# The output projections and the q transposes of a decode-attention kernel, regrouped: wider tiles, two PSUM banks, two copying engines

## The chip, the cores and the metric

The kernel runs on one core of one Trainium2 chip. The metric is the device time of one execution, in microseconds (us); lower is better. "Span" is the time between the first and the last instruction in the profile; in the fast runs of most kernels here the device time is 1.2 to 1.3 us longer than the span. Engine names in the profile are PE (TensorE matmuls), PEld (TensorE weight loads), DVE (VectorE), ACT (ScalarE), POOL (GpSimd) and SP (SyncE, which issues the DMAs).

## The reference, cut to what matters

Two independent attention layers, A and B, decode one token for a batch of 8 against a long cache. Their outputs stand side by side.

```python
# per layer: x (8,1,1024), k_cache and v_cache (8,32,4096,128), wq (1024,4096), wo (4096,1024), all bf16
q      = (x @ wq).reshape(B, Sq, H, Dh)            # then (B, H, Sq, Dh)
scores = einsum("bhqd,bhkd->bhqk", q, k_cache) * Dh ** -0.5
p      = softmax(scores)
o      = einsum("bhqk,bhkd->bhqd", p, v_cache)
y      = o.transpose(0, 2, 1, 3).reshape(B, Sq, H * Dh) @ wo      # (8, 1, 1024)
out    = concatenate([y_A, y_B], axis=-1)                        # (8, 1, 2048)
```

Nearly all the traffic is the four caches: the profile counts 1107 MB read from memory.

## The kernel before

A ring of three large buffers in on-chip memory receives tiles of k, v and the weights. VectorE multiplies and folds k tiles, TensorE sums them and applies the probabilities to v. At the head, q is projected and transposed; at the end, the two outputs are projected with `wo`. The change touches only the head and the end.

The transposes of q, four groups of eight rows per layer, each with its own small copy:

```python
def make_qT(c):
    for hb in range(HB):                                   # HB = 4
        rows = slice(32 * hb, 32 * hb + B)
        def emit(e, rows=rows):
            for j in range(HQ):                            # HQ = 8
                i = e.transpose(misc_bf16[:, j * B:(j + 1) * B], q_sb[rows, c, j * Dh:(j + 1) * Dh], ident[rows, rows],
                                tile_position=(rows.start, 0))
            return i
        op = add("pe", emit, [opQs[(c, hb, 0)], opQs[(c, hb, 1)], ...])
        opQT[c] = opQT["last"] = add("dve", ...tensor_copy(...), [op])
```

The output projection. Four column tiles of TensorE work side by side on 256 columns each: in the trace of the first projection four matmuls start every 109 ns at full clock and every 213 ns at half, while one takes 363 ns (the page's mean for this line, both projections). The weights of the second projection arrive in four cuts, of 20, 8, 3 and 1 rows of 4 column tiles, so that only a little work is left after the last cut lands:

```python
wo_cuts = ((0, 20), (20, H - 4), (H - 4, H - 1), (H - 1, H))
...
def make_proj(c):
    w = tile_of("wo", c)
    for i, (r0, r1) in enumerate(wo_cuts if c == NC - 1 else ((0, H),)):
        def emit(e, r0=r0, r1=r1):
            for r in range(r0, r1):
                for q in range(NT):                        # NT = 4, DT = 256
                    col = r * D + q * DT
                    x = e.matmul(proj[32 * q:32 * (q + 1), 0:DT], on_sb[:, c, r:r + H * B:HQ],
                                 w[:, col:col + DT], start=(r == 0), stop=(r == H - 1), tile_position=(0, 32 * q))
            return x
        opProj[c] = add("pe", emit, [opNorm[c], opT[("wo", c, i)], c_pad, opEv.get(c - 1)])
    opEv[c] = add("dve", lambda e: e.tensor_copy(orow[:, c, :], proj[:, 0:DT]), [opProj[c]])
    outs.append(dma(out[...], orow[0:128:32 // B, c, :], ...))
```

Each matmul here is a pair of instructions, a weight load and the matmul itself. The first projection has 128 pairs, the second 128: 80, 32, 12 and 4 in its cuts.

## Time and profile before

| | before |
|---|---|
| device time, median | 2563.53 us |
| span of the profiled execution | 2562.3 us |
| memory traffic | 432 GB/s over the span |
| VectorE busy | 85% |
| last weights landed to end of span | about 2.7 us (2562.3 - 2559.62) |

The page of the profiled execution first gives each engine's busy time and share, then, in 40 equal slices of the span, the busy tenths of the DMA engines. The third kind of line is a group of instructions: line, engine, operation, output and input tile, shape, count | busy us, mean ns of one | idle time just before them, and what ended most of it.

```profile
span 2562.3 us, 18832 instructions
...
PE 1115.7 (44%) x7712; PEld 396.7 (15%) x7712; DVE 2170.6 (85%) x1042; ACT 129.9 (5%) x401; POOL 2.6 (0%) x15
...
DMA  9999999999999999999999999999999999999999
...
L330 DVE TENSOR_TENSOR ring<-ring,qbc 128x8192 bf16<-128x8192 bf16 x256 | 1131.7, 4421 | 310.9 <-DMA ring<-in_A_k_cache_dram 158.0
...
L305 DVE COPY qT<-misc 128x64 bf16<-128x64 bf16 x8 | 3.5, 436 | 17.6 <-PE misc L301 17.6
```

The DMA engines are full in every slice (9 in all 40). VectorE, the busiest compute engine, waits 310.9 us for k tiles, so it has room. The same is read from a long middle stretch, in the view by windows (stretch in us, its length, then busy us and count of PE, PEld, DVE, ACT and POOL; mean granted clock of TensorE, DMA share, GB/s):

```profile
2000.00:2500.00 500.00, 221.85 (x1464) 76.61 (x1462) 436.54 (x208) 23.98 (x77) 0.00 (x0) 0.67 1.00 433
```

At the end, the timeline of TensorE and VectorE (start us, duration us, then the group; in brackets the idle time before it and what ended it):

```profile
2540.13 5.49 PE L431 MATMUL proj<-ring,on_sb 128*32 128x256 bf16 x128 [9.92 <-DMA ring<-in_A_wo_dram]
...
2552.35 4.50 PE L431 MATMUL proj<-ring,on_sb 128*32 128x256 bf16 x80 [6.73 <-DMA ring<-in_B_wo_dram]
...
2557.16 1.22 PE L431 MATMUL proj<-ring,on_sb 128*32 128x256 bf16 x32 [0.31 <-DMA ring<-in_B_wo_dram]
```

Every part of the second projection waits for its cut of weights: TensorE is done with one cut before the next lands. The chain that ended last (start us, us, what) says the same of the very end:

```profile
2519.89 39.72 DMA ring<-in_B_wo_dram
2559.62 0.04 issue
2559.66 0.36 PE proj L431 x4
2560.03 0.02 issue
2560.05 0.42 DVE orow L435
```

The last cut landed at 2559.62 us; four matmuls, one copy of 0.42 us, and the output DMA, issued at 2560.50 us, follow it.

### The profile page before, as it was taken

Reading aid. Unit: us, or ns where it says so; the run is one execution under the profiler, and the core shown is the slowest. Engines: PE = TensorE matmul, PEld = TensorE weight load, DVE = VectorE, ACT = ScalarE, POOL = GpSimd, SP = SyncE. Lnnn points to the kernel's source line nnn. Section 1 sums busy time; section 2 is a strip of 40 time slices with the busy share of each in tenths; the row PEclk is TensorE's granted clock in tenths of the full one; section 3 lists DMA queues with packets and bytes.
Section 4 is the critical chain, followed back from the end, with each engine's and each line's share of the span. In section 5 each row is a group of like instructions: output and inputs, shape, how many; then the busy total and the mean of one; then the engine's idle time right before and its main releaser. Section 6 shows DMA issues by size and latency. Waiting matters only on the chain.

```text
span 2562.3 us, 18832 instructions
## 1 busy us (share of the span) xinstructions
PE 1115.7 (44%) x7712; PEld 396.7 (15%) x7712; DVE 2170.6 (85%) x1042; ACT 129.9 (5%) x401; POOL 2.6 (0%) x15
## 2 busy tenths in 40 slices
PE   2443443443443443444444444434444434434434
PEld 1111111111111111111111111111111111111112
DVE  3898898898898898898898888988988988988983
ACT  1100000000000000000000000000000000000000
POOL 0000000000000000000000000000000000000000
PEclk7676766767767767766666766767667666767667
DMA  9999999999999999999999999999999999999999
GB/s 425 427 438 430 437 431 436 432 436 432 435 431 437 430 438 430 435 432 435 433 431 437 431 435 433 434 433 435 433 435 433 435 433 435 433 435 433 435 433 394
DMA packets 19554, 1107.51 MB, mean 432 GB/s; under 512 B 2184, under 2 KB 2248, under 8 KB 2520
## 3 DMA queue, kind: packets, MB, share of 16 engines
q1 hardware_dynamic: 19512, 1107.34, 99.9%
q8 instruction: 7, 0.11, 0.0%
q10 hardware_dynamic: 32, 0.03, 0.0%
q14 instruction: 3, 0.02, 0.0%
HBM read 1107.33 MB, written 0.03 MB: 432 GB/s over the span
## 4 chain that ended last, share of the span: by engine, by line
DMA 52%; DVE 28%; issue 16%; PE 4%; ACT 0%; another core or an unknown queue 0%; DVEq 0%; SPq 0%
DMA ring<-in_A_k_cache_dram 25%; DMA ring<-in_B_k_cache_dram 25%; DVE ring L330 10%; DVE ring L335 10%; PE red L345 4%; DVE s_sb L353 4%; DVE PM L370 3%; DMA ring<-in_B_wo_dram 2%; DVE rmax L359 1%; DVE rtmp L360 0%; ACT PM L291 0%; DVEq L135 0%; DVE ngm L363 0%; PE o L285 0%
## 5 line engine op out<-in xcount | busy, mean ns | idle before, releaser
L330 DVE TENSOR_TENSOR ring<-ring,qbc 128x8192 bf16<-128x8192 bf16 x256 | 1131.7, 4421 | 310.9 <-DMA ring<-in_A_k_cache_dram 158.0
L345 PE MATMUL red<-ring,ident 128*128 128x512 bf16 x2048 | 780.1, 550 | 1392.7 <-DVE ring L335 1392.7
L335 DVE TENSOR_TENSOR ring<-ring 128x4096 bf16<-128x4096 bf16 x256 | 582.3, 2274 | 0.0
L345 PEld LDWEIGHTS red<-ring,ident 128*128 128x128 bf16 x2048 | 238.5, 127 | 1842.6 <-DVE ring L335 1495.2
L353 DVE TENSOR_REDUCE s_sb<-red 128x64 f32<-128x1024 f32 x256 | 312.0, 1219 | 2.9 <-PE red L345 2.9
L382 PE MATMUL pv<-ring,PM 128*32 128x512 bf16 x4096 | 274.4, 415 | 4.6 <-DVE PM L370 4.6
L370 DVE TENSOR_TENSOR PM<-pe,own_h 128x2048 bf16<-128x2048 bf16 x64 | 146.2, 2284 | 0.7 <-ACT pe L365 0.7
L382 PEld LDWEIGHTS pv<-ring,PM 128*32 128x32 bf16 x4096 | 103.9, 104 | 188.4 <-issue 116.2
L319 ACT ACTIVATE qbc<-misc 128x128 bf16<-128x128 f32 x64 | 17.8, 278 | 1093.4 <-PE misc L317 1093.4
L365 ACT ACTIVATE pe<-s_sb,ngm 128x256 bf16<-128x256 f32 x64 | 32.5, 508 | 470.2 <-DVE ngm L363 470.2
L390 ACT ACTIVATE accS<-pv 128x512 bf16<-128x512 f32 x64 | 38.2, 597 | 350.5 <-PE pv L382 350.5
L399 PEld LDWEIGHTS o<-accS,E 128*32 128x32 bf16 x1024 | 31.3, 100 | 49.3 <-issue 48.1
L399 PE MATMUL o<-accS,E 128*32 128x32 bf16 x1024 | 38.1, 185 | 0.7 <-ACT accS L390 0.7
L405 ACT ACTIVATE o_sb<-o 32x32 f32 (+1 forms) x64 | 11.9, 186 | 449.5 <-PE o L399 448.9
L359 DVE TENSOR_REDUCE rmax<-s_sb 128x1 f32<-128x256 f32 x64 | 26.9, 420 | 2.2
L435 DVE CAST orow<-proj 128x256 bf16<-128x256 f32 x2 | 0.8, 424 | 28.7 <-PE proj L431 28.7
L431 PE MATMUL proj<-ring,on_sb 128*32 128x256 bf16 x256 | 12.1, 363 | 17.7 <-DMA ring<-in_A_wo_dram 9.9
L312 ACT ACTIVATE qst<-qT 128x128 bf16 (+1 forms) x64 | 18.7, 293 | 2.0 <-DVE qT L305 2.0
L305 DVE COPY qT<-misc 128x64 bf16<-128x64 bf16 x8 | 3.5, 436 | 17.6 <-PE misc L301 17.6
L360 DVE TENSOR_SCALAR rtmp<-half,rmax 128x32 f32<-128x32 f32 x64 | 15.4, 241 | 2.2
L363 DVE TRANSPOSE_TENSOR_REDUCE ngm<-rtmp 128x1 f32<-128x32 f32 x64 | 13.5, 211 | 2.2
L317 PE MATMUL misc<-ident,qst 128*128 128x128 bf16 x64 | 14.8, 232 | 0.9 <-ACT qst L312 0.9
(33 smaller groups left out, 65.5 us busy)
## 6 DMA issues: line engine op xcount, KB each, us to landing
ring<-in_B_wo_dram SPq DMA_DIRECT2D x1, 5120.0 KB, 33.6
ring<-in_B_wo_dram SPq DMA_DIRECT2D x1, 2048.0 KB, 38.2
ring<-in_B_wo_dram SPq DMA_DIRECT2D x1, 768.0 KB, 39.6
ring<-in_A_k_cache_dram SPq DMA_DIRECT2D x32, 40.0
ring<-in_A_v_cache_dram SPq DMA_DIRECT2D x32, 27.8
ring<-in_B_k_cache_dram SPq DMA_DIRECT2D x32, 39.8
ring<-in_B_v_cache_dram SPq DMA_DIRECT2D x32, 27.8
ring<-in_B_wo_dram SPq DMA_DIRECT2D x1, 256.0 KB, 39.7
```

What stands on the lines that cost most here:

```text
L312: return e.activation(qst[:, n % 2, :].rearrange("p (j m) -> p j m", m=MP), from_.unsqueeze(2).to_broadcast([128, HQ, MP]), ACTF.Copy)
L319: opQbc[n] = add("act", lambda e: e.activation(qbc[:, n % 2, :], misc[:, 0:Dh], ACTF.Copy), [opQb[n], _at(opMul, NR * (n - 2) + NR - 1)])
L330: opMul[s] = add("dve", lambda e: e.tensor_tensor(v, v, qbc[:, n % 2, :].unsqueeze(1).to_broadcast([128, CT, Dh]), ALU.mult), [opT[("k", n ...
L335: return add("dve", lambda e: e.tensor_tensor(v[:, :, 0:64], v[:, :, 0:64], v[:, :, 64:128], ALU.add), [opMul[s]])
L345: i = e.matmul(dst, ident[:], v[:, g, :, j, :], start=(j == 0), stop=(j == 3))
L353: opRed[s] = add("dve", lambda e: e.tensor_reduce(s_sb[:, n % 2, r * CT:(r + 1) * CT], red_ps[s % 2][:, :].rearrange("p (t w) -> p t w", w ...
L359: m = add("dve", lambda e: e.tensor_reduce(rmax[:], s_sb[:, n % 2, :], AX.X, ALU.max), [opRed[NR * n + NR - 1]])
L365: opExp[n] = add("act", lambda e, at: e.activation(pe[:], s_sb[:, n % 2, :], ACTF.Exp, bias=ngm[:, n % 2:n % 2 + 1], scale=scale, accum_ou ...
L370: opPM[n] = add("dve", lambda e: e.tensor_tensor(PM[:], pe[:].unsqueeze(2).to_broadcast([128, T, HQ]), own_h[:].unsqueeze(1).to_broadcast( ...
L382: i = e.matmul(pv_ps[32 * q:32 * (q + 1), :], PM[:, t:t + 4, :].rearrange("p t j -> p (t j)"), v[:, t * Dh:(t + 4) * Dh], start=(g == 0), ...
L390: opAcc[n] = add("act", lambda e: e.activation(accS[:], pv_ps[:], ACTF.Copy), [opPV[n], _at(opExt, n - 1)])
L399: x = e.matmul(to, E[:, i, PH - 1 - u:PH - 1 - u + MB], accS[:, i * 128 + H * u:i * 128 + H * (u + 1)], start=(i == 0 and u == 0), stop=(i ...
```

## The change

The intent has three parts.

1. Head: the four groups of q transposes of 8 rows become one group of eight transposes of 104 rows (the rows of all four groups, with unused rows between them), and one copy in place of four. The unused rows are cleared first, by a memset of `PM` on GpSimd.
2. First projection: 2 column tiles of 512 columns instead of 4 of 256. It has time to spare (done at 2545.62 us, with the next weights in use from 2552.35), so its slower form should cost nothing; half as many instructions.
3. Second projection: each column tile's 256 columns are split over two PSUM banks of 128, so that VectorE copies the first bank and ScalarE the second at the same time.

The diff, cut to its core:

```diff
+        c_PM = add("pool", lambda e: e.memset(PM[:], 0.0))
...
-                                           [opQ[(c, f)]])
+                                           [opQ[(c, f)], c_PM])
...
         def make_qT(c):
-            for hb in range(HB):
-                rows = slice(32 * hb, 32 * hb + B)
-                ...                      # 8 transposes of 8 rows and one copy of 64 columns, per group
+            rows = 32 * (HB - 1) + B
+            def emit(e):
+                for j in range(HQ):
+                    i = e.transpose(misc_bf16[:, j * 128:j * 128 + rows], q_sb[0:rows, c, j * Dh:(j + 1) * Dh], ident[0:rows, 0:rows])
+                return i
+            op = add("pe", emit, [opQs[(c, hb, f)] for hb in range(HB) for f in range(2)] + [...])
+            opQT[c] = opQT["last"] = add("dve", ...one tensor_copy of all groups..., [op])
...
         def make_proj(c):
+            last = c == NC - 1
+            nt = NT if last else NT // 2
+            dt = D // nt
+            banks = (proj, pv_ps) if last else (proj,)
+            fw = dt // len(banks)
+            for i, (r0, r1) in enumerate(wo_cuts if last else ((0, H),)):
+                for f, bank in enumerate(banks):
+                    def emit(e, r0=r0, r1=r1, f=f, bank=bank):
+                        for r in range(r0, r1):
+                            for q in range(nt):
+                                col = r * D + q * dt + f * fw
+                                x = e.matmul(bank[32 * q:32 * (q + 1), 0:fw], on_sb[:, c, r:r + H * B:HQ],
+                                             w[:, col:col + fw], start=(r == 0), stop=(r == H - 1), tile_position=(0, 32 * q))
+                        return x
+                    opProj[(c, f)] = add("pe", emit, [opNorm[c], opT[("wo", c, i)], c_pad, opAcc[NQ - 1]] + opEv.get(c - 1, []))
+            rows, to = 32 * nt, orow if last else accS
+            opEv[c] = [add("dve", lambda e: e.tensor_copy(to[0:rows, 0:fw], proj[0:rows, 0:fw]), [opProj[(c, 0)]])]
+            if last:
+                opEv[c].append(add("act", lambda e: e.activation(to[:, fw:dt], pv_ps[:, 0:fw], ACTF.Copy), [opProj[(c, 1)]]))
```

More of the change, by code (lines that the diff above doesn't have):

```diff
@@ L186, in _build_kernel @@
         on_sb = sb("on_sb", [128, NC, B * H + H], BF16)
-        orow = sb("orow", [128, NC, DT], BF16)
+        orow = sb("orow", [128, DT], BF16)
         q_sb = PM[:].rearrange("p t j -> p (t j)").rearrange("p (c n) -> p c n", c=NC)
@@ L291, in make_q @@
                     opQs[(c, hb, f)] = add("act", lambda e, rows=rows, f=f: e.activation(q_sb[rows, c, f * 512:(f + 1) * 512], q_ps[f][rows, :], ACTF.Copy),
-                                           [opQ[(c, f)]])
+                                           [opQ[(c, f)], c_PM])
             opUse[("wq", c)] = opQ[(c, 1)]
         def make_qT(c):
-            for hb in range(HB):
-                rows = slice(32 * hb, 32 * hb + B)
-                def emit(e, rows=rows):
-                    for j in range(HQ):
-                        i = e.transpose(misc_bf16[:, j * B:(j + 1) * B], q_sb[rows, c, j * Dh:(j + 1) * Dh], ident[rows, rows],
-                                        tile_position=(rows.start, 0))
-                    return i
-                op = add("pe", emit, [opQs[(c, hb, 0)], opQs[(c, hb, 1)], c_ident, c_xT, opQT.get("last"), opQbc.get(0), opQbc.get(1)])
-                opQT[c] = opQT["last"] = add("dve", lambda e, hb=hb: e.tensor_copy(
-                    qT[:, c].rearrange("p (b h) -> p h b", h=H)[:, hb * HQ:(hb + 1) * HQ, :],
-                    misc_bf16[:, 0:HQ * B].rearrange("p (j b) -> p j b", b=B)), [op])
+            rows = 32 * (HB - 1) + B
[3 more added lines that the diff above has]
+                return i
+            op = add("pe", emit, [opQs[(c, hb, f)] for hb in range(HB) for f in range(2)]
+                     + [c_ident, c_xT, opQT.get("last"), opQbc.get(0), opQbc.get(1)])
+            opQT[c] = opQT["last"] = add("dve", lambda e: e.tensor_copy(
+                qT[:, c].rearrange("p (b g j) -> p j g b", g=HB, j=HQ),
+                misc_bf16[:, 0:HQ * 128].rearrange("p (j g w) -> p j g w", g=HB, w=32)[:, :, :, 0:B]), [op])
         def make_stage(n):
@@ L424, in make_proj @@
             w = tile_of("wo", c)
-            for i, (r0, r1) in enumerate(wo_cuts if c == NC - 1 else ((0, H),)):
-                def emit(e, r0=r0, r1=r1):
-                    for r in range(r0, r1):
-                        for q in range(NT):
-                            col = r * D + q * DT
-                            x = e.matmul(proj[32 * q:32 * (q + 1), 0:DT], on_sb[:, c, r:r + H * B:HQ],
-                                         w[:, col:col + DT], start=(r == 0), stop=(r == H - 1), tile_position=(0, 32 * q))
-                    return x
-                opProj[c] = add("pe", emit, [opNorm[c], opT[("wo", c, i)], c_pad, opEv.get(c - 1)])
@@ L435, in make_proj @@
-            opEv[c] = add("dve", lambda e: e.tensor_copy(orow[:, c, :], proj[:, 0:DT]), [opProj[c]])
-            outs.append(dma(out[:, 0, c * D:(c + 1) * D].rearrange("b (q n) -> q b n", q=NT), orow[0:128:32 // B, c, :],
-                            ("out", 0), [opEv[c]] if c == NC - 1 else [opEv[c], opT[("wo", NC - 1, len(wo_cuts) - 2)]], "sp"))
+            last = c == NC - 1
+            nt = NT if last else NT // 2
+            dt = D // nt
+            banks = (proj, pv_ps) if last else (proj,)
@@ new lines, in make_proj @@
+            rows, to = 32 * nt, orow if last else accS
+            opEv[c] = [add("dve", lambda e: e.tensor_copy(to[0:rows, 0:fw], proj[0:rows, 0:fw]), [opProj[(c, 0)]])]
+            if last:
+                opEv[c].append(add("act", lambda e: e.activation(to[:, fw:dt], pv_ps[:, 0:fw], ACTF.Copy), [opProj[(c, 1)]]))
+            outs.append(dma(out[:, 0, c * D:(c + 1) * D].rearrange("b (q n) -> q b n", q=nt), to[0:rows:32 // B, 0:dt],
+                            ("out", 0), opEv[c] if last else opEv[c] + [opT[("wo", NC - 1, len(wo_cuts) - 2)]], "sp"))
```

## The prediction

> **What bounds the kernel now.** The DMA queue. The page's slices show DMA at 9 tenths in all 40 slices, 432 GB/s over the span of 2562.3 us. The view by windows gives 433 to 434 GB/s in every long stretch from 140 to 2500 us. VectorE is busy 85% and idles 310.9 us waiting for k tiles. Transfers are issued far ahead: a k tile takes 40.0 us from issue to landing, a v tile 27.8, while the queue needs about 19.4 us for one (8.39 MB at 433 GB/s, an estimate). So work before 2500 us counts only if it delays an issue by more than that lead.
>
> **Head.** Four groups of small transposes and copies per input (0.35 us on TensorE and 0.43 us on VectorE each, 29.9 to 33.6 us) become eight transposes and one copy. For input A q is ready 1 to 3 us earlier, but the first multiply waits for its k tile until 43.48 us. For input B (74.1 to 77.9 us) the release of the k slot (issue at 80.93 us) moves by under 1 us, with about 20 us of transfers still queued. The copy grows from 64 elements (0.43 us) to 256: I estimate 0.5 to 1.4 us. The added memset of PM on GpSimd I estimate at 1.8 us: memsets of 1 and 140 elements took 0.10 and 0.21 us, 0.8 ns per element, times 2048. It delays the load of x (issued at 2.49 us), hence the B_wq issue at 16.89 us by some 2 us; the queue is full until about 42 us. Worth zero.
>
> **First projection.** It runs 2540.13 to 2545.6 us; the next weights land at 2552.3 us. Now 4 column tiles of 256 start every 213 ns at clock 0.5 and 109 ns at 1.0. With 2 tiles of 512, 32 groups at 427 then 216 ns: about 9 us (estimate), done near 2549. If the clock never rose, 13.7 us, delaying the second projection by 1.5 us. [...] Its output leaves only at 2559.07, as before. Worth zero.
>
> **Second projection and tail.** Twice as many matmuls of half the width: the same streaming time, if weight loads keep up (the small extraction matmuls show 27 ns spacing on one tile). After the last cut lands: matmuls at 2559.66, copy from 2560.05 (0.42 us), output issue at 2560.50, landing about 1.8 us later. Now the two copies of 128 columns take about 0.29 us (VectorE, estimate) and 0.28 us (ScalarE, a 128x128 copy in the trace), the second bank's matmuls finishing about 0.05 us after the first's. Gain 0.1 to 0.2 us, the only part on the last chain.
>
> **Predicted: 2563.4 us** (before 2563.53), 8 in 10 between 2562.3 and 2564.6. Faster by over 2%: 0.005; within 2%: 0.985; slower: 0.01.
>
> **Right if** DMA stays at 9 in all slices at 432 GB/s; the first k multiply starts near 43.5 us; the first projection lasts 8 to 10 us and ends before 2552; the last cut lands near 2559.7; the last two copies take under 0.3 us side by side.
>
> **Wrong if** changed issue times disturb the DMA stream; the narrow matmuls are bound by weight loads and run past the last landings; the clock is low at the end; or x arrives so late that it delays a k issue.

2563.53 us before, less the expected gain of 0.1 to 0.2 us, with zero for the head and for the first projection, comes to the predicted 2563.4. The clock that the estimate of about 9 us for the first projection supposes is that of the trace before: 0.5 from its start at 2540.13 until 2543.84 us, then 1.0 until 2550.67. At the prediction's spacings that is 9 groups at 427 ns and 23 at 216, or 8.8 us (an estimate from these figures).

## The result, and the profile after

| | before | after |
|---|---|---|
| device time, median (range) | 2563.53 us (2563.44 to 2563.78, 6 runs) | 2564.56 us (2563.51 to 2564.79, 6 runs) |
| ratio, after over before | | 1.0003, 95% interval 0.999 to 1.0016 |
| span of the profiled execution | 2562.3 us | 2563.5 us |

A ratio here is the mean time of one kernel's runs over that of the other's runs of the same rounds, so it is not quite the ratio of the medians. By the 2% measure the two are the same. But the six runs of the new kernel are not one cluster: four lie at 2564.4 to 2564.8 us and two at 2563.5 to 2563.6 us, in both cases with a span about 1.2 us shorter than the time. Something costs about 1 us in most executions, at a place where the change was meant to gain 0.1 us. The rest of this document is about that microsecond.

The page of the kernel after. The DMA slices are as before, the VectorE multiplies too; the eight copies of 0.436 us are two of 1.274 us. The line of queue q8 gives its packets, MB and share; it is used further down:

```profile
DMA  9999999999999999999999999999999999999999
...
q8 instruction: 7, 0.11, 0.0%
...
L330 DVE TENSOR_TENSOR ring<-ring,qbc 128x8192 bf16<-128x8192 bf16 x256 | 1131.0, 4418 | 310.4 <-DMA ring<-in_A_k_cache_dram 157.2
...
L305 DVE COPY qT<-misc 128x256 bf16<-128x256 bf16 x2 | 2.5, 1274 | 17.2 <-PE misc L301 17.2
```

The timeline at the end of the kernel after. `proj` is the first bank, `pv` the second:

```profile
2540.20 9.25 PE L437 MATMUL proj<-ring,on_sb 128*32 128x512 bf16 x64 [9.61 <-DMA ring<-in_A_wo_dram]
...
2552.41 1.47 PE L437 MATMUL proj<-ring,on_sb 128*32 128x128 bf16 x80 [2.96 <-DMA ring<-in_B_wo_dram]
...
2553.69 1.44 PE L437 MATMUL pv<-ring,on_sb 128*32 128x128 bf16 x79
2558.52 0.27 PE L437 MATMUL pv<-ring,on_sb 128*32 128x128 bf16 x1 [3.40 <-issue]
```

The first projection does what was predicted. The second starts with its weights, runs 80 matmuls of the first bank and 79 of the second in 2.7 us, and then stands still for 3.4 us, one matmul before the end of the first cut. "issue" means that the engine waited for nothing that the profile shows: no semaphore, no data. By the time the 80th matmul starts, at 2558.52 us, the second cut has long landed (in the kernel before its matmuls wait for it and start at 2557.16 us). The chain that ended last is now this:

```profile
2518.60 33.68 DMA ring<-in_B_wo_dram
...
2553.88 1.24 PE pv L437 x77
2555.12 3.40 issue
2558.52 0.27 PE pv L437
2558.78 0.85 PE proj L437 x32
2559.64 0.85 PE pv L437 x32
...
2561.24 0.12 PE pv L437 x4
2561.36 0.02 issue
2561.38 0.28 ACT orow L444
```

The last link from memory in it is the first cut, landed at 2552.28 us, not the last one, which landed at 2559.67 us (2559.62 before; the transfers were not disturbed). After the gap, 97 pairs are still to be run, and TensorE no longer waits for data, it is behind. The two copies are as short as predicted, 0.29 and 0.28 us side by side, but they start 1.2 to 1.3 us later than the one copy of before (2561.28 and 2561.38 against 2560.05 us).

One more line of the trace matters. The queue q8, which carries instructions and no data, moves a packet of 16384 bytes in that gap. TensorE's compiled program is 124032 bytes for 1938 instructions, 64 bytes each, so a packet is 256 instructions. The packets are put down to TensorE because the compiled programs of the other engines have 160 instructions at most. The last such packets of each kernel (in us, start and end, in the trace's record of DMA packets):

```
before   2543.91-2544.92   2556.34-2557.36
after    2530.87-2531.96   2555.88-2556.90   2559.57-2560.44
```

In the kernel before, one packet comes during the first projection and one during the second, and TensorE stalls at neither. In the kernel after, none comes during the first projection (2540 to 2549 us), and one comes within the gap.

The head of the kernel, timeline of the kernel before and then of the kernel after (the last copy of q before, then the copy that hands out q to all partitions):

```profile
33.17 0.43 DVE L305 COPY qT<-misc 128x64 bf16<-128x64 bf16 x1 [0.54 <-PE misc L301]
...
34.33 0.28 ACT L319 ACTIVATE qbc<-misc 128x128 bf16<-128x128 f32 x1 [0.38 <-PE misc L317]
```

```profile
32.23 0.78 PE L301 MATMUL misc<-ident,PM 104*128 104x104 bf16 x8 [2.54 <-ACT PM L292]
33.05 1.27 DVE L305 COPY qT<-misc 128x256 bf16<-128x256 bf16 x1 [13.46 <-PE misc L301]
...
35.05 0.28 ACT L319 ACTIVATE qbc<-misc 128x128 bf16<-128x128 f32 x1 [0.38 <-PE misc L317]
```

### The profile page after: what moved, and what is told of

It is laid out like the page before. It is cut to its first block, busy times and chain, and to the rows that moved or that the text cites. A ratio compares the mean times of both kernels' runs of the same rounds, so it can differ in the third digit from the quotient of the medians.

```text
span 2563.5 us, 18856 instructions
## 1 busy us (share of the span) xinstructions
PE 1121.8 (44%) x7728; PEld 396.7 (15%) x7728; DVE 2169.4 (85%) x1036; ACT 130.1 (5%) x402; POOL 4.3 (0%) x16
## 4 chain that ended last, share of the span: by engine, by line
DMA 51%; DVE 28%; issue 16%; PE 5%; another core or an unknown queue 0%; ACT 0%; DVEq 0%; SPq 0%
DMA ring<-in_A_k_cache_dram 25%; DMA ring<-in_B_k_cache_dram 25%; DVE ring L330 10%; DVE ring L335 10%; PE red L345 4%; DVE s_sb L353 4%; DVE PM L370 3%; DMA ring<-in_B_wo_dram 1%; DVE rmax L359 1%; DVE rtmp L360 0%; ACT PM L292 0%; PE pv L437 0%; DVEq L135 0%; PE proj L437 0%
## 5 line engine op out<-in xcount | busy, mean ns | idle before, releaser
L437 PE MATMUL proj<-ring,on_sb 128*32 128x128 bf16 (+1 forms) x192 | 12.8, 327 | 12.6 <-DMA ring<-in_A_wo_dram 9.6
L363 DVE TRANSPOSE_TENSOR_REDUCE ngm<-rtmp 128x1 f32<-128x32 f32 x64 | 13.5, 211 | 2.2
```

## The experiments

### The theories

The main theory, called the fetch theory below: TensorE's own program comes to it in the packets of q8, blocks of 256 instructions. The packet of a block starts about when TensorE comes to the block ahead of it, and where that block is done before the packet has landed, TensorE stands at its end. This was the author's guess from the gap in the kernel after, whose packet ends at 2556.90 us, 1.62 us before TensorE goes on; the runs have to show it, and the cost with it. The kernel before runs 256 instructions of the second projection in about 7.7 us (2552.35 to 2560.02), part of it waiting for data. The kernel after has 512 instructions in the same place, and no block boundary in the first projection, so that the boundaries fall where the instructions go fastest (a pair every 16 ns).

The rivals: (a) the narrow matmuls are bound by their weight loads; (b) the clock of TensorE alone makes the difference; (c) writing two PSUM banks, one of them read last by ScalarE, makes TensorE wait; (d) the change at the head or in the first projection disturbs the transfers.

The fetch theory can be tested sharply, because instructions can be counted. In the compiled program of the kernel after, counted from zero, the first projection has the instructions 1287 to 1414, the instruction 1415 is a wait for the first cut of weights that stands alone, and the first cut's pairs have 1416 to 1735 (first bank to 1575, second bank from 1576). One constant is not known: where in the kernel's own instructions the first boundary lies. The gap of the kernel after fixes it at 199 (256 less 57), which puts block boundaries at 1479, 1735 and 1991. That is one fitted number, from one trace. Every later place of a gap is then predicted with no further freedom. In the kernel before, the boundary at 1479 lies inside the first projection (1389 to 1644) and that at 1735 at the 90th of the 256 instructions of the second (1646 to 1901), so TensorE came to the block ahead of it during the first. The traces hold as many matmuls and weight loads as the compiled programs run (7728 of each in the kernel after), so a boundary can also be put on the time axis.

A dummy pair, used as padding below, is a tiny matmul into a PSUM bank whose last reader is done. It moves all later instructions by two:

```python
e.matmul(red_ps[0][0:32, 0:8], ident[:, 0:32], ident[:, 0:8], start=True, stop=True, tile_position=(0, 0))
```

### e1: the kernel after, unaltered

No edit.

> The changed kernel unaltered, as a control on this chip. Theory F (instruction fetch): TensorE runs dry at the 256-instruction block boundary that falls on the last matmul of the second projection's first cut. The gap of 3.4 us (last start 2554.90, next 2558.52) comes back at the same instruction, with an instruction DMA of 16384 bytes ending 1 to 2 us before it ends; times 2563.4 to 2564.9, in two groups (2563.5 and 2564.7) as before, the lower group where the clock after the gap is 1.0 and not 0.5. Rival W (weights): the gap is a wait for the second cut's landing, and moves with that landing. Rival N (narrow matmuls are simply slower): no gap of over 1 us without a wait is needed to explain the time.

Measured: 2564.49 us (2563.32 to 2564.66, five runs, one of them in the faster group), ratio 1.0003 (0.9989 to 1.0016). The timeline of the profiled run of e1:

```profile
2554.31 1.84 PE L437 MATMUL pv<-ring,on_sb 128*32 128x128 bf16 x79
2558.33 0.22 PE L437 MATMUL pv<-ring,on_sb 128*32 128x128 bf16 x1 [2.18 <-issue]
```

The gap is at the same matmul and ends within 0.2 us of the same time, though it is 1.2 us shorter: here the clock was at half at first, the first bank's 80 matmuls took 2.36 us instead of 1.47, and the gap began later. So the end of the gap is not set by what TensorE did before it. That rules out rival (a): a bound by weight loads would show as slow pairs, not as one stop, and the pairs before the stop run 16 ns apart at full clock (80 in 1.28 us, from 2552.41 to 2553.69 in the kernel after). It also answers the first half of rival (b): the stop is there at full clock (after) and at half (e1), so the clock does not make it. What the clock does after it is shown further down.

### e2 and e3: padding ahead of the first projection

```diff
         make_norm(1)
+        def emit_pad(e):
+            for _ in range(28):                 # e3: 4
+                x = e.matmul(...dummy pair...)
+            return x
+        add("pe", emit_pad, [opPM[n], c_ident])
         make_proj(0)
```

> The changed kernel with 28 dummy weight-load and matmul pairs (56 instructions) put in TensorE's idle time before the first projection, so that the block boundary falls 7 instructions into the second projection[...]. Theory F: no gap over 1 us without a semaphore wait in the second projection (there may be a short one, under 1.2 us, that ends before the second cut lands at 2557.2); last matmuls right after the last cut lands near 2559.7; span 2562.0 to 2562.3, time 2563.2 to 2563.5 in all runs, 1.1 us under the slow group of the changed kernel. Rivals W and N: nothing changes but 1 us more of idle-time work; time stays 2563.5 to 2564.8.

> The same with 4 dummy pairs (8 instructions). Theory F: the gap stays 3 to 4 us long but falls 8 instructions earlier in the program: five matmuls of the first cut follow it where one did; time as the changed kernel. Rivals W and N: the gap, if any, stays before the last matmul of the first cut.

Measured: e2 2565.64 us (2564.93 to 2565.85), ratio 1.0008 (0.9995 to 1.0022); e3 2563.66 us (2563.53 to 2564.33, four runs), ratio 1.0001 (0.9986 to 1.0017). The timelines of e2 and of e3:

```profile
2554.35 1.45 PE L437 MATMUL pv<-ring,on_sb 128*32 128x128 bf16 x51
2558.17 0.66 PE L437 MATMUL pv<-ring,on_sb 128*32 128x128 bf16 x29 [2.37 <-issue]
```

```profile
2553.87 2.32 PE L437 MATMUL pv<-ring,on_sb 128*32 128x128 bf16 x75
2558.45 0.29 PE L437 MATMUL pv<-ring,on_sb 128*32 128x128 bf16 x5 [2.25 <-issue]
```

The place is what the count says: 28 pairs earlier than the 79th is the 51st, 4 pairs earlier is the 75th. The gap follows the instruction count, while banks, tiles, data and shapes of the projections are those of the kernel after. That rules out rival (c).

The time of e2 missed: I had expected 2563.2 to 2563.5 us, because its boundary lies only 8 instructions beyond the wait for the first cut, and I supposed that the packet would come while TensorE still waited. It did not: the packet started at 2555.77 us, 3.67 us after the landing of the first cut. The gap ended when it always does, and 28 more pairs were left after it: at the 27 ns per pair of the half clock (0.85 us for 32 in the kernel after) that is 0.75 us (an estimate from these traces), about the 1 us by which e2 is slower than e1.

### e4, e7 and e8: one part of the change each

e4 has the projections of the kernel after with the head of the kernel before; e7 only the new head; e8 only the new first projection, with the second as before.

```diff
 # e4: before.py + make_proj and orow of the kernel after
 # e7: before.py + c_PM and make_qT of the kernel after
 # e8: before.py, in make_proj:
+            nt = NT if last else NT // 2
+            dt = D // nt
-                        for q in range(NT):
-                            col = r * D + q * DT
-                            x = e.matmul(proj[32 * q:32 * (q + 1), 0:DT], ...)
+                        for q in range(nt):
+                            col = r * D + q * dt
+                            x = e.matmul(proj[32 * q:32 * (q + 1), 0:dt], ...)
```

> The kernel before with only the two projections changed; head, q transposes and memset as before. TensorE's program is 102 instructions longer before the projections than in the changed kernel, so the boundaries fall at instruction 90 of the first projection, at 217 of 320 in the first cut of the second, and at 25 of 48 in its third cut. Theory F: no gap in the first cut [...]; a gap without a semaphore wait after the 25th instruction of the third cut (its first bank's 12 matmuls are done, the second bank's are not), from about 2559.3 to 2559.6 or later, up to 2560.3; time 2563.5 to 2564.4. Rivals W and N: no gap inside the third cut. If the head's changes cost the time, this kernel is at 2563.4 with no gap.

> The head's change alone (q transposes of 104 rows, the memset), projections as before: all of the second projection is 256 instructions. Every theory that puts the loss in the tail expects 2563.4 to 2563.7, as before, with no gap. If the later load of x or the memset costs time, it is slower.

> The first projection alone in 2 column tiles of 512, second projection and head as before. Expected 2563.4 to 2563.7, no gap; the first projection lasts 8.4 to 9.9 us in place of 5.5 and ends before 2550.5.

Measured: e4 2563.63 us (2563.45 to 2563.78), e7 2563.54 us (2563.39 to 2563.80), e8 2563.60 us (2563.44 to 2563.78, four runs); all three have a ratio of 1.0. So the head and the first projection alone cost nothing, which rules out rival (d). The surprise is e4, which has the whole new end and no loss. The head counts nonetheless, by its number of instructions: with the old head the boundaries fall elsewhere, in the third cut. The timeline of e4:

```profile
2559.03 0.41 PE L437 MATMUL proj<-ring,on_sb 128*32 128x128 bf16 x12 [0.62 <-DMA ring<-in_B_wo_dram]
2559.65 0.41 PE L437 MATMUL pv<-ring,on_sb 128*32 128x128 bf16 x12 [0.21 <-issue]
```

There is a gap "issue", at the place counted beforehand, after the 12 first-bank matmuls of the third cut. It ends at 2559.65 us, when the last cut lands anyway, so it costs next to nothing. The instruction packets were at 2548.50 us, during the first projection, and at 2557.10 us. It is a matter of where the boundaries fall.

### e5: the boundary 8 instructions behind a wait in a weight load

```diff
         make_norm(1)
+        make_pad(27, [opPM[n], c_ident])
         make_proj(0)
+        make_pad(1, opEv[0])
         make_proj(1)
```

The pad after the first projection takes over the wait for VectorE's copy. In the kernel after, the first pair of the second projection has two waits, for VectorE and for the DMA, and the compiled program has one of them, that for the DMA, as an instruction of its own in front of the weight load. With the pad, the wait for the DMA is inside the weight load, and the boundary is again 8 instructions beyond it, as in e2. In e2, with the wait an instruction of its own, the packet started only at 2555.77 us; e5 asks whether it comes earlier without that.

> As the kernel with 28 dummy pairs, but 27 stand before the first projection and one after it; that one waits for VectorE's copy of the first projection, so that the second projection's first weight load waits for its DMA alone. In the trace of the last run with 28 pairs the DMA wait was a semaphore instruction of its own, after which TensorE's program was fetched no further (the instruction DMA started 3.6 us after the wait ended, though the boundary lay 8 instructions on), and the wait on VectorE was part of the weight load. Theory F, refined [...]: the instruction DMA now starts between 2550 and 2555 us, before the first cut lands; no gap over 1.5 us without a wait, and none after the second cut's landing at 2557.1; last matmuls start within 0.1 us of the last landing near 2559.6; time 2563.2 to 2563.5 in all runs, 0.1 us under the kernel before. If the standalone wait is not what held the fetch, the gap is back after 50 or so matmuls of the second bank and the time is 2564.9 to 2565.9 as with 28 pairs before.

Measured: 2563.62 us (2563.48 to 2563.77), ratio 1.0001 (0.9987 to 1.0014); before in the same rounds 2563.48 us (2563.28 to 2563.71). The timeline of e5:

```profile
2552.41 2.36 PE L437 MATMUL proj<-ring,on_sb 128*32 128x128 bf16 x80 [1.99 <-DMA ring<-in_B_wo_dram]
2554.56 1.65 PE L437 MATMUL pv<-ring,on_sb 128*32 128x128 bf16 x80
2557.15 0.72 PE L437 MATMUL proj<-ring,on_sb 128*32 128x128 bf16 x32 [0.94 <-DMA ring<-in_B_wo_dram]
...
2560.04 0.28 ACT L444 ACTIVATE orow<-pv 128x128 bf16<-128x128 f32 x1 [28.71 <-PE pv L437]
```

No gap. The instruction packet moved to 2550.17-2551.19 us, before the first cut had landed, and even before the pad's own wait ended. All four cuts wait for their data again, and the two copies start at 2559.98 and 2560.04 us. This is the kernel that the change had intended: its output DMA is issued at 2560.39 us against 2560.50 us before, which is the predicted gain of 0.1 us at that point. But its runs are not faster than those of before (2563.62 against 2563.48 us, the intervals overlap). So I found no version that beats both kernels; 0.1 us cannot be told from the spread of 0.4 us between runs. In e5, and in e2, the time is also 1.4 to 1.5 us longer than the span, where it is 1.2 to 1.3 us in the kernel before. In both, the boundary at 1991 falls among the last ten instructions of TensorE's program; whether that is the reason was not tested.

e2 and e5 together also say something of the wait's form. With the boundary 8 instructions away, the packet started at 2550.17 us, 2.2 us before the second projection's first matmul (2552.41), where the wait was inside the weight load (e5), and at 2555.77 us, 3.5 us after that matmul (2552.24), where it stood alone (e2).

### e9 and e10: the boundary farther behind the wait

```diff
         make_proj(0)
+        make_pad(9, opEv[0])                    # e10: make_pad(1, opEv[0])
         make_proj(1)
```

Both have the wait inside the weight load; the boundary is 46 instructions beyond it in e9 and 62 in e10.

> As the kernel with 27 pairs before and one after the first projection, but with 9 pairs after it and none before: a shorter program, with the boundary 46 instructions beyond the weight load that waits for the first cut. Theory F: [...] the instruction DMA starts before 2552 us, there is no gap over 1.5 us, and the last matmuls start within 0.15 us of the last landing. Time 2563.3 to 2563.6: the changed kernel's loss of 1 us is gone, and the gain of 0.1 us over the kernel before may or may not show. If the fetch does not run 46 instructions ahead of a waiting load, the gap of 2.4 to 3.6 us is back, 17 instructions before the end of the first cut, with 2563.6 to 2564.7.

> The same with one pair in place of nine: the only difference to the changed kernel is that the DMA wait before the second projection is part of the weight load and not an instruction of its own (one dummy pair takes the wait for VectorE). The boundary is 62 instructions beyond the waiting load. Theory F: as above if the fetch runs 62 instructions ahead (the instruction DMA starts before 2552 us, time 2563.3 to 2563.6); otherwise the gap comes back two instructions before the end of the first cut and the time is 2563.5 to 2564.7.

Measured: e9 2564.83 us (2563.90 to 2564.96), ratio 1.0004; e10 2564.51 us (2563.48 to 2565.06, four runs), ratio 1.0005. The timelines of e9 and of e10:

```profile
2554.53 1.85 PE L437 MATMUL pv<-ring,on_sb 128*32 128x128 bf16 x71
2558.68 0.40 PE L437 MATMUL pv<-ring,on_sb 128*32 128x128 bf16 x9 [2.30 <-issue]
```

```profile
2553.82 2.34 PE L437 MATMUL pv<-ring,on_sb 128*32 128x128 bf16 x79
2558.23 0.27 PE L437 MATMUL pv<-ring,on_sb 128*32 128x128 bf16 x1 [2.07 <-issue]
```

Both have the gap, where the count puts it (after 71 and 79), and as late as ever. So with the wait inside the weight load the packet came early where the boundary was 8 instructions behind it (2550.17 us in e5), and not where it was 46 or 62 (2556.04 us in e9, 2555.79 in e10). What lies between was not tried, and what sets the distance is not shown.

### e6 and e11: the length of the program

```diff
 # e6: the kernel after
-            nt = NT if last else NT // 2
+            nt = NT
 # e11: the kernel before, 77 dummy pairs ahead of the first projection
+        make_pad(77, [opPM[n], c_ident])
         make_proj(0)
```

e6 keeps four column tiles in the first projection, so that a boundary falls inside it again, and the next one in the second cut. e11 gives the kernel before as many TensorE instructions in all (2066) as e6 has.

> The changed kernel with the first projection in 4 column tiles of 256 as before, and the second in two banks. The boundary now falls before the last matmul of the second cut (its 128th instruction). Theory F: no gap in the first cut; one before the last matmul of the second cut that ends between 2559.1 and 2559.8; time 2563.4 to 2564.3. Rivals (the second bank, or ScalarE's copy, costs the time): the gap would stay where it was or not be there.

> The kernel before, with 77 dummy pairs in TensorE's idle time before the first projection, which makes its TensorE program as long (2066 instructions) as that of the run with the second projection alone. That run ended its span at 2562.3 us, as early as the kernel before, but took 2564.7 us, 1 us more outside the span, with an instruction DMA after the span's end. If the program's length is the cause, this kernel takes 2564.3 to 2564.8 us with a span of 2562.3 us, and has an instruction DMA after 2562.3 us. If not, 2563.4 to 2563.6 us.

Measured: e6 2564.77 us (2564.63 to 2565.02, four runs), ratio 1.0005; e11 2563.43 us (2563.27 to 2563.50), ratio 1.0. The timeline of e6:

```profile
2557.65 0.68 PE L437 MATMUL pv<-ring,on_sb 128*32 128x128 bf16 x31
2559.41 0.22 PE L437 MATMUL pv<-ring,on_sb 128*32 128x128 bf16 x1 [1.08 <-issue]
```

Again the gap is at the counted place, the last matmul of the second cut. It ends at 2559.41 us, before the last cut lands, and the span of e6 is 2562.3 us, that of before. Yet its profiled run took 2564.67 us, 2.4 us more than its span instead of 1.2 to 1.3. So e6 is slow for another reason, which lies after the last instruction of the profile. In its trace one more instruction packet stands at 2563.64 to 2564.97 us, after the span, as in no other kernel; that may be it. A program of that length is not the cause by itself: e11 is as long, and does not show it. The trace of e11 has an eighth instruction packet too, at 2558.17 to 2559.10 us and so inside its span, where the shorter programs have seven. What sets e6 apart is thus when the eighth comes. This stays open.

### What the fetch costs

The times of the first cut's landing, of the instruction packet and of the end of the gap, in the kernels that stall in the first cut (us, from the traces' records of DMA packets and of matmuls; the last column is resume minus landing):

```
kernel   landing    packet              TensorE resumes   landing to resume
after    2552.28    2555.88-2556.90     2558.52           6.24
e1       2552.06    2555.72-2556.74     2558.33           6.27
e2       2552.10    2555.77-2556.79     2558.17           6.07
e3       2552.14    2555.90-2556.93     2558.45           6.31
e9       2552.34    2556.04-2557.07     2558.68           6.34
e10      2552.13    2555.79-2556.81     2558.23           6.10
```

From the landing of the data to the first instruction of the next block it takes 6.1 to 6.3 us, of which the packet itself is 1.0 us: it starts 3.6 to 3.8 us after the landing, and TensorE goes on 1.4 to 1.6 us after its end. The landing is not yet the block, for the boundary at 1479 lies 8 to 63 instructions behind the wait. The first instruction executed in the block starts at 2552.88 us in the kernel after, and at 2552.92, 2552.25, 2552.66, 2552.84 and 2552.61 us in e1, e2, e3, e9 and e10: the next block follows 5.4 to 5.9 us later. In e4 and e6, which stand in a later cut, it is 4.6 and 4.7 us (2555.04 to 2559.65 and 2554.74 to 2559.41 us). A block must therefore last at least some 4.6 to 5.9 us here, 36 to 46 ns for each of its 128 pairs (an estimate from these traces). The pairs of 128 columns take 16 ns at full clock (80 in 1.28 us) and 27 ns at half (32 in 0.85 us), so such a block lasts 2.0 or 3.4 us and stalls at either clock. The pairs of 256 columns take 27 and 53 ns (four in 109 and in 213 ns): 3.5 or 6.8 us. In the kernel before they were also spread out by the waits for data.

The next packet came only about 1 us after TensorE resumed (2559.57 us in the kernel after), when the weight transfers were nearly over. Whether the full data queues are what delays the packets at 2555.9 us is not shown; no experiment here varied it. In e4 and e8 the blocks at 1479 are entered during the first projection, with the weight transfers still running: there the packet starts 1.0 us after the first instruction of the block (2548.50 against 2547.51 us) and 0.1 us before it (2547.24 against 2547.31 us). In e5 the packet starts at 2550.17 us, just before VectorE's copy ends (2549.51 + 0.68 = 2550.19 us) and lets the pad start. So that packet did not wait for the pad's weight load to get what it waited for. What starts a packet, the traces do not show.

### Why the same kernel runs in two groups

e1 and e10 have the gap at the same matmul, ending within 0.1 us of each other, and the same pairs left. Yet e1's span is 2563.2 us and e10's 2562.2. The windows after the gap (columns as above; the third-last is the clock), e1 and then e10:

```profile
2558.30:2560.00 1.70, 1.67 (x73) 1.67 (x76) 0.00 (x0) 0.00 (x0) 0.00 (x0) 0.61 0.19 64
```

```profile
2558.30:2560.00 1.70, 1.70 (x97) 1.58 (x97) 0.00 (x0) 0.00 (x0) 0.00 (x0) 1.00 0.19 65
```

In e1 the clock falls to half at 2558.68 us, and only 73 of the matmuls left fall in that stretch; in e10 it stays at full, and all 97 do. In the kernel after it was at half from 2558.24 to 2561.65 us. The clock records of the kernels before and after hold only 0.5 and 1.0 (125 stretches of each before, 128 after), and every stretch but the last one lasts 3.41 us or a whole multiple of it. So the loss has two parts that come together: the gap, which leaves 97 or more pairs to the end, and the clock, which decides how long these take. Where the clock stays full, they are done about when the last cut lands anyway: the output DMA is issued at 2560.42 us in e10 and at 2560.61 us in e3, against 2560.50 us before. Where it is at half, the issue comes at 2561.34 us (e1) to 2561.77 us (e9). Of the profiled runs, those with the low clock after the gap (after, e1, e2, e9) took 2564.5 to 2564.9 us, those with the full clock (e3, e10) 2563.5 to 2563.7. For the runs that were timed and not profiled, the same division is an inference. No profiled run has the low clock there and no gap, so the clock alone was not tested; but none of the 33 timed runs of the kernel before took over 2563.82 us, and none of e4 or e5 over 2563.78 us. Whether the gap is what let the clock fall is not shown: e10 has a gap too (2.07 us), and its clock stays at 1.00 from 2558.30 to 2561.00 us.

## Why the prediction was right or wrong

The total was predicted at 2563.4 us with a range of 2562.3 to 2564.6; the median is 2564.56, inside the range by 0.04 us, with three of the six runs above it (2564.70 to 2564.79 us), and "within 2%" holds. That the median is inside is luck: the sum had no term for the loss. The sign of the small difference was wrong: 0.1 us of gain was expected, and the medians differ by 1.03 us of loss.

- "The DMA queue" bounds the kernel: right. The slices and the GB/s are the same after, and the last cut landed at 2559.67 us as against 2559.62.
- "Worth zero" for the head: right (e7, ratio 1.0), as was the memset, estimated at 1.8 us and measured at 1.80 us. The copy was given 0.5 to 1.4 us and took 1.27. Inside it one step was wrong: "For input A q is ready 1 to 3 us earlier". It was ready 0.7 us later (35.05 against 34.33 us), for two reasons. The eight copies of ScalarE ended 0.5 us later (32.18 against 31.68 us). And one group of transposes has to wait for all of them, until 32.23 us, where the four small groups had overlapped with them, so that nothing was gained after them: 2.87 us from their end to that copy against 2.65 us. It cost nothing, since the first k multiply waited until 43.46 us (43.48 before).
- "Worth zero" for the first projection: right in its own time (9.25 us measured, about 9 estimated; e8, ratio 1.0). What the prediction overlooked is that half as many instructions move a block boundary out of it and into the second.
- "The same streaming time, if weight loads keep up": this is the step that failed. The weight loads nearly kept up: 16 ns per pair at full clock, where half of the 27 ns of a pair of 256 columns would be 13.5, and 27 ns at half clock against half of 53. What did not keep up was the supply of instructions: twice as many of them for the same data, at a place where 256 of them last 2.0 to 3.4 us and 256 more take 4.6 to 5.9 us to come. The term was put at zero; it measured 2.4 to 3.6 us of standing still from the start of one matmul to the start of the next, of which about 1 us reaches the end of the kernel where the clock is at half afterwards, and next to nothing where it is full (e3, e10).
- "Gain 0.1 to 0.2 us" at the tail: right as a mechanism (two copies of 0.29 and 0.28 us), and shown without the stall by e5, where the output is issued 0.11 us earlier. In the kernel after it is lost to the gap and the low clock behind it. Among what would make the prediction wrong it had "the clock is low at the end", which did happen, and it did not have the fetch.

What stays open: e6's extra microsecond after the span, the extra 0.2 us of e2 and e5 there, what starts a packet and whether the data traffic delays it, and at what distance between 8 and 46 instructions behind the wait it no longer comes early.

## What to carry to other kernels

Halving the width of matmuls doubled the instructions here, and TensorE outran the supply of its own program: its pairs took 16 to 27 ns, and the next block came 36 to 46 ns per pair after the start of the one ahead (the estimate above). Where a timeline shows a wait "issue" in the middle of a straight run of equal instructions, look for a 16384-byte instruction packet in it and count instructions to the block boundary, which came every 256 instructions here (gaps at 1735 in the kernel after and at 1991 in e4 and e6; where the first one lies had to be fitted). If the stretch after a long wait is the critical one, keep it short in instructions, or move the boundary by a few dummy instructions. In e5 it took two things, a boundary within 8 instructions of the wait and a wait that does not stand alone; either without the other (e2, e9, e10) did not help. The place shifted with every edit to TensorE's program, the head's included (102 instructions in e4 moved it from the first cut to the third), so test each part together with the whole. A slow stretch with time to spare may have been hiding a fetch: here the first projection of the kernel before, with its packet at 2543.91-2544.92 us and no stall.
